# Transposes by matmul instead of by DMA, and buffer fills on the sync engine's queue, in a four-layer attention kernel ordered by a planner

## The chip, the cores and the metric

The kernel runs on one core of a Trainium2 chip. The core has TensorE (PE), VectorE (DVE), ScalarE (ACT), GpSimd (POOL) and the sync engine (SP); 16 DMA engines move data for all of them. A DMA issued by GpSimd goes to a software queue, one issued by the sync engine to a hardware queue. The metric is the device time of one execution in microseconds, as the median of several runs.

## The reference

Four layers run one after the other over x of 2048 rows by 512 columns in bf16: softmax attention A (32 query heads of width 16 that share one key and one value head), linear attention B, A again, B again. Each layer adds its output to x.

```python
def _A_ref(x, wq, wk, wv, wo):
    q = (x @ wq).reshape(B, S, H, Dh).transpose(0, 2, 1, 3)
    k = x @ wk
    v = x @ wv
    scores = jnp.einsum("bhqd,bkd->bhqk", q, k) * (Dh ** -0.5)
    p = _softmax(scores, axis=-1)
    o = jnp.einsum("bhqk,bkd->bhqd", p, v)
    return o.transpose(0, 2, 1, 3).reshape(B, S, H * Dh) @ wo
...
def _B_ref(x, wqkv, wo):
    ...
    phi = lambda t: jnp.where(t > 0, t + 1, jnp.exp(t)) + 1e-6
    pq, pk = phi(q), phi(k)
    kv = jnp.einsum("bhsd,bhse->bhde", pk, v)
    z = jnp.einsum("bhsd->bhd", pk)
    num = jnp.einsum("bhqd,bhde->bhqe", pq, kv)
    den = jnp.einsum("bhqd,bhd->bhq", pq, z)[..., None] + 1e-6
    ...
x = x + _A_ref(_layernorm(x, axis=-1), A_wq, A_wk, A_wv, A_wo)
x = x + _B_ref(_layernorm(x, axis=-1), B_wqkv, B_wo)
x = x + _A_ref(_layernorm(x, axis=-1), A_wq, A_wk, A_wv, A_wo)
x = x + _B_ref(_layernorm(x, axis=-1), B_wqkv, B_wo)
```

## The kernel before

The 2048 rows are 16 tiles of 128. All of x and the weights stay on the core.

**Attention (layers 0 and 2).** The scores of one tile of queries, half of the heads and one tile of keys are made in blocks of 128 by 512; a layer has 2048 blocks. A score matmul (`qk_mm`, L983) uses a quarter of TensorE's rows, so three or four blocks run side by side into PSUM banks. The exponential of a block is made on one of two engines:

- ScalarE takes most blocks, two or three at a time (L1163, the "doubles" and "triples" 128x1024 and 128x1536).
- VectorE takes the others by integer arithmetic: it adds a constant to the score and writes it as int16, whose bits read as bf16 are a power of two with a linear mantissa (L1249, one "block"). To mend the linear mantissa, three more copies of the block are wanted, each with another small constant added to the int16 (L1297, the "additions"), and the product with the values uses all four with four weights. Blocks are gathered by four into a "set" (`FB`, 128x2048), so an addition works on four blocks at once.

One of a set's three additions can be done by DMA instead of by VectorE: `prime` (L1309) fills a free buffer with the constant by a DMA that reads the row `shift_row` from DRAM (L1321, a "fill"), and `dma_shift` (L1328) later adds the set to it by an accumulating DMA (L1330). Both are issued by GpSimd. Whether a set goes that way is decided in `dve_shifts` (L1277): a fill must stand ready, the end of the layer must be more than `DMIN` segments away, and the planner's DMA backlog must be below `DQ`. A fill is started when fewer than `NPRE` stand ready and more than `FBP` buffers are free. Buffers lent by other tensors (`xn`, `wq`, `wo2`, `OBB`, `sacc`) serve as `FB` too, so a fill can have those names; the order prints `wo2` as `wo`.

The product with the values (L1037) reads what either engine or the DMA has made and sums in one PSUM bank. TensorE fills its gaps with matmuls that multiply by zeros (L1082 and L969, the "fillers"). At the end of a tile the sum is normalised into `Osb`, turned (`epilogue`, L1420) and projected (L754).

**Linear attention (layers 1 and 3).** Each tile of x is normalised (`ln_tile`, L826) into `xn`, turned into `xnT` and projected. Most of this runs beside the attention layer before it, as soon as that layer's tile is done.

**Turning a tile** is done in one of two ways. `dmat` (L760) issues a DMA transpose on the sync engine's queue. Or TensorE multiplies by the identity (L862 for `xn`, L1442 for `Osb`, four matmuls a tile) and ScalarE or VectorE copies the result from PSUM (L739). `FARA`, `FARB` and `FARO` say for which tiles the DMA is used.

**The order.** `Planner` (L36) simulates the engines with the costs written at each operation, and what comes out is each engine's fixed order of instructions; on the chip an engine runs its own order and waits on semaphores. A DMA's landing is modelled by one queue (`dmaq`, L193 to L203). While a transpose is under way no fill and no addition by DMA is dispatched (L158), and those that follow wait for the last transposes (L200):

```python
            if o.port and self.port > self.now or o.xfer and self.turning:
                held.append(x)
                continue
...
            if o.xfer:
                o.deps.update(self.turned)
                self.dmaq = max(end, self.dmaq) + o.xfer[0]
                end = self.dmaq + o.xfer[1]
```

`TUNE` replaces constants of the planner at the start of layer 0 and of layer 2.

Of the kernel before, what the change touches and what calls it, by code (L numbers as in the profile page):

```python
# [8 lines left out]
I16 = mybir.dt.int16  # L9
# [3 lines left out]
PE, AC, DV, PO, SP = "pe", "act", "dve", "pool", "sp"  # L13
ENGS = (PE, AC, DV, PO, SP)

P = 128
# [19 lines left out]
class Planner:  # L36
# [43 lines left out]
    def op(self, opts, reads=(), writes=(), prio=5.0, lat=0.08, dma=False, name="", join=None, mode="full", port=False, after=(), behind=(), xfer=None, trn=False):  # L80

        o = Op()
        o.opts, o.prio, o.users, o.done, o.end = opts, prio, [], False, None
        o.eng, o.fn, o.n, o.value, o.sem, o.signal, o.isdma = None, None, None, None, None, False, dma
        o.name = (name, lat)
        o.freed = False
        o.begun = None
        o.cols = 0
        o.mode = mode
        o.port = port  # L90
        o.xfer = xfer
        o.trn = trn
        deps = set()
        for k in reads:
            deps.update(self.ws(k))
        for k in list(writes) + list(after) + list(behind):
            deps.update(self.ws(k))
            deps.update(self.readers.get(k, ()))
        if join is not None:
            deps.update(join.deps)  # L100
            deps.discard(join)
        for k in writes:
            if join is not None and join in self.ws(k):
                self.writer[k] = self.ws(k) + [o]
            else:
                self.writer[k] = [o]
                self.readers[k] = []
        for k in list(reads) + list(after):
            if k not in writes:
                self.readers.setdefault(k, []).append(o)  # L110
        o.deps = deps
        o.left = 0
        chain = len(opts) == 1 and PE in opts
        for d in deps:
            if not (d.done or (chain and d.freed and d.eng == PE)):
                o.left += 1
                d.users.append(o)
        if o.left == 0:
            self._eligible(o)
        return o  # L120
# [26 lines left out]
    def _dispatch1(self, e):  # L147
# [4 lines left out]
        while h:  # L152
# [9 lines left out]
            if w:  # L162
                held.append(x)
                self.at(w, lambda: self._dispatch(e))
                break
            if e == PE and STICK and o.mode != "row" and o.mode != self.mode != "row":
                like = [y for y in h if y[2].eng is None and y[2].mode == self.mode and y[0] <= o.prio + STICK]
                if like:
# [187 lines left out]
class Seg:  # L356
# [11 lines left out]
    def take(self, js, back=False):  # L368
# [33 lines left out]
TRS = 1.4  # L402
TRT = 1.0
FARA = (4, 16)
FARB = 12
FARO = 12
FARM = {1: (), 3: ()}
GROW = (5,)
BLS = 1.4
BLO = 5.0  # L410
DXB = 2.0
# [13 lines left out]
ENDL = 12  # L425
# [6 lines left out]
CHB = 4  # L432
FBO = 2
FBS = 4
AHEAD = 20
CHT = 19
PSH = False
STICK = 1.5
PBL = 1.2
BACK = 2  # L440
PRING = 8
# [1 line left out]
DMIN = 4  # L443
NPRE = 2
EVEN = True
CHE = 8
AVOID = True
PGEN = 0.95
DPF = 1.75
DXF = 3.3  # L450
DTAIL = 2.0
DQ = 4.0
FBP = 4
TUNE = {0: {"CHE": 2, "CHT": 26, "FBP": 3, "ENDL": 16, "STICK": 0.8},
        2: {"CHE": 2, "FBO": 1, "AHEAD": 26, "BLS": 2.3, "DXB": 1.2, "NPRE": 3, "DMIN": 3, "STICK": 0.8}}


def bass_interleave_layers__grouped_kv_mqa__linear_attn_block__prompt_kernel(
# [12 lines left out]
    op = pl.op  # L471
# [39 lines left out]
    FB = sb("FB", [P, NFB, CHB * 512], BF16)  # L511
# [23 lines left out]
    pts, fbs = {}, {}  # L535
# [28 lines left out]
    def once(tag, keys):  # L564
        if tag in seen:
            return ()
        seen.add(tag)
        return keys

    def guest(L, kind, i, h=None):  # L570
        return once((L, kind, i, h), home[kind, i]) if (kind, i) in home else ()
# [10 lines left out]
    def bank_bf(i):  # L582
        return ps[:, i * 512:(i + 1) * 512].bitcast(BF16)[:, 0:512].rearrange("p (a b) -> p a b", a=4)
# [119 lines left out]
    cst = nc.dram_tensor("shift_row", (1, CHB * 512), I16, kind="Internal").ap()  # L703

    def fb_keys(i):
        return [("FB", i, h) for h in range(CHB)]
# [53 lines left out]
    def dmat(dst, src, reads, writes, prio, after=()):  # L760
        return op({SP: (0.1, lambda e: e.dma_start(dst, src, transpose=True))}, reads=reads, writes=writes, prio=prio, lat=0.5, dma=True, behind=after, trn=True)

    def until(*keys):
        for k in keys:
            yield ("ops", pl.ws(k))

    def halves(bs, dst, key, prio, psrc=None, after=()):
        l = op({DV: (DH_DUR, lambda e: e.tensor_copy(dst(0), psrc(bs[0], 0)))}, writes=[B_(bs[0]), key], prio=prio, behind=after)
        r = op({AC: (AH_DUR, lambda e: e.copy(dst(1), psrc(bs[1], 1)))}, writes=[B_(bs[1]), key], prio=prio, join=l, behind=after)
        pl.give_after(banks, bs[0], [l])  # L770
        pl.give_after(banks, bs[1], [r])
        return [l, r]
# [50 lines left out]
    def ring(L, t):  # L823
        return t % 4 if L == 3 else t
# [149 lines left out]
    def run_a(L):  # L974
# [23 lines left out]
        def spend(h, o):  # L998
            h[0] -= 1
            if o not in h[1]:  # L1000
                h[1].append(o)
            if h[0] == 0:
                pl.give_after(h[2], h[3], h[1])
# [85 lines left out]
        def act_stream():  # L1089
            if L == 0:  # L1090
                globals().update(TUNE[0])
            yield ("flag", ("K", L, 0))
            globals().update(TUNE[L])
            if L:
# [214 lines left out]
        def prime():  # L1309
            yield ("flag", ("K", L, T - 1))  # L1310
            if L == 0:
                row = FB[0:1, NFB - 1, :].bitcast(I16)
                op({DV: (0.6, lambda e: e.memset(row, DSH * 128 // NSH))}, writes=fb_keys(NFB - 1), prio=1.0)
                op({SP: (0.54, lambda e: e.dma_start(cst, row))}, reads=fb_keys(NFB - 1), writes=["cst"], prio=1.0, lat=2.5, dma=True)
            yield from until("cst")
            while state["si"] < len(segs) - DMIN:
                if len(primed) >= NPRE or len(fb_pool.free) <= FBP or fb_pool.wait:
                    yield ("sleep", 0.2)
                    continue
                g_ = yield ("acq", fb_pool, 9.0)  # L1320
                o = op({PO: (PGEN, lambda e, g_=g_: e.dma_start(fbs[g_].bitcast(I16), cst.to_broadcast([P, CHB * 512])))}, reads=["cst"], writes=fb_keys(g_), prio=9.0,  # L1321
                       lat=0.3, dma=True, behind=guest(L, "FB", g_), xfer=(DPF, DTAIL))
                primed.append((g_, o))
            while primed:
                g_, o = primed.pop()
                pl.give_after(fb_pool, g_, [o])

        def dma_shift(blk, f_, hold, g_, o):  # L1328
            pl.stat["dma"] += 1
            o = op({PO: (PGEN, lambda e: e.dma_start(fbs[g_].bitcast(I16), fbs[f_].bitcast(I16), accum_op=ALU.add))}, reads=fb_keys(f_), writes=fb_keys(g_), prio=0.0, lat=0.3,  # L1330
                   dma=True, xfer=(DXF, DTAIL))
            spend(hold, o)
# [32 lines left out]

        pl.process(spare())
        pl.process(prime())
        for i in pairs:
            pl.process(spare_sacc(i))
# [50 lines left out]
        def epilogue(t):  # L1420
# [5 lines left out]
            rd = [("Osb", k, 0), ("Osb", k, 1)]  # L1426
            if t >= FARO or t in ECRIT:
                yield from until(*rd)
            if t in ECRIT:
                bs = yield from acq2(pr)  # L1430
                o = tr2(src, rd, bs, pr)
                halves(bs, lambda h: dst[:, 2 * h:2 * h + 2, :], ("OT", m), pr, lambda b, h: bank_bf(b)[:, 0:2, :])
            elif t < FARO:
                o = dmat(dst, src, rd, [("OT", m)], pr)
# [50 lines left out]
    def run_b(L):  # L1485
# [45 lines left out]
        def tile_(t):  # L1531
            pr = base(t) + 0.01 * t
            yield ("flag", ("x", L - 1, t))
            yield from ln_tile(L, t, pr, t < FARB, t in ECRIT)
            c = ring(L, t)
# [398 lines left out]
```

## Time and profile before

| | us |
|---|---|
| median of 3 runs | 1499.13 |
| lowest and highest | 1496.74 and 1501.04 |
| the profiled execution | 1500.94 |
| its span, first to last instruction | 1499.2 |
| busy: ScalarE, TensorE, VectorE, GpSimd | 1448.2, 1424.7, 1406.7, 358.7 |

The profile is of one execution. Busy time is the time in which at least one instruction of the engine is under way; instructions of an engine overlap a little at their ends, so a row's mean duration is longer than the distance from one start to the next. An idle time in a row's brackets is that of the engine just before the row, with what ended it. A transpose or load on the sync engine's queue is written SPq. The stages by time: layer 0's attention to about 715 us with layer 1 partly beside it, the rest of layer 1 and the start of layer 2 to about 840 us, layer 2's attention with layer 3 beside it to about 1461 us, then the rest of layer 3.

### The profile page before, as it was taken

The page shows a single profiled execution, that of the slowest core. Times are in us where ns is not written, and L with a number is a line of the kernel's source. Part 1 is how long each engine was busy: PE and PEld are TensorE (multiplying, and loading weights), DVE is VectorE, ACT ScalarE, POOL GpSimd, SP SyncE. Part 2 cuts the span into 40 slices and gives each one's busy share as a digit, 9 for nine tenths or more (in the row PEclk, how much of TensorE's full clock was granted, in tenths as well). Part 3 has the DMA queues.
Part 4 walks back from the last instruction along what each step waited for, and adds up shares of the span by engine and source line. Part 5 has one row for each costly group of instructions (what it writes and reads, how often), then busy time and mean ns, then how long its engine had stood idle before and what let it go on. Part 6 is the DMA issues. An engine that isn't in the chain of part 4 may idle for free. (4 is left out here: it accounts for less than half of the span.)

```text
span 1499.2 us, 40089 instructions
## 1 busy us (share of the span) xinstructions
PE 1424.7 (95%) x16261; PEld 511.2 (34%) x16261; DVE 1406.7 (94%) x2594; ACT 1448.2 (97%) x1510; POOL 358.7 (24%) x537
## 2 busy tenths in 40 slices
PE   7999999989999999999999999999899999999998
PEld 4433332323233323333644333333233323333335
DVE  7999989989999999999767799999999999999996
ACT  8999999989999999999699999999999999999996
POOL 5322222212232222100111222222222223223001
PEclk9999999999999999999999999999999999999999
DMA  5867777767668878500000577586976877788101
GB/s 118 222 163 150 153 161 174 155 134 170 143 159 186 183 153 200 121 30 2 1 2 1 128 173 156 138 177 156 169 169 155 183 150 174 173 177 209 33 2 57
DMA packets 91480, 200.81 MB, mean 134 GB/s; under 512 B 39713, under 2 KB 46369, under 8 KB 91298
## 3 DMA queue, kind: packets, MB, share of 16 engines
q0 software_dynamic: 49968, 181.95, 53.1%
q1 hardware_dynamic: 41330, 16.30, 5.6%
q8 instruction: 130, 2.13, 0.6%
q14 instruction: 52, 0.43, 0.1%
HBM read 98.60 MB, written 2.10 MB: 67 GB/s over the span
## 5 line engine op out<-in xcount | busy, mean ns | idle before, releaser
L1163 ACT ACTIVATE PT<-ps 128x1024 bf16<-128x1024 f32 (+1 forms) x947 | 1002.4, 1171 | 8.2 <-PE ps L983 6.6
L983 PE MATMUL ps<-QT,KM 32*128 32x512 bf16 x4096 | 538.5, 385 | 21.8 <-ACT PT L1163 12.1
L1249 DVE TENSOR_SCALAR FB<-ps 128x512 int16<-128x512 f32 x785 | 515.2, 679 | 17.7 <-PE ps L983 16.9
L1037 PE MATMUL ps<-FB,VW 128*32 128x512 bf16 x3179 | 431.3, 385 | 12.5 <-DVE sacc L1383 2.8
L1037 PE MATMUL ps<-PT,V 128*32 128x512 bf16 x2109 | 349.1, 387 | 17.9 <-ACT PT L1163 7.5
L983 PEld LDWEIGHTS ps<-QT,KM 32*128 32x128 bf16 x4096 | 135.2, 91 | 443.6 <-ACT PT L1163 205.0
L1163 ACT ACTIVATE xnT<-ps 128x1024 bf16<-128x1024 f32 (+1 forms) x235 | 249.5, 1136 | 3.3 <-PE ps L983 2.8
L1297 DVE TENSOR_SCALAR FB<-FB 128x2048 int16<-128x2048 int16 (+1 forms) x331 | 220.3, 674 | 0.6
L1163 ACT ACTIVATE OBB<-ps 128x1024 bf16<-128x1024 f32 (+1 forms) x166 | 183.7, 1164 | 8.2 <-PE ps L983 8.0
L1330 POOL DMA_DIRECT2D FB<-FB x89 | 88.6, 1005 | 329.4 <-DVE FB L1249 179.6
L1082 PE MATMUL ps<-QT,V 128*32 128x512 bf16 (+6 forms) x680 | 161.9, 317 | 0.5 <-DVE FB L1249 0.5
L1037 PEld LDWEIGHTS ps<-FB,VW 128*32 128x32 bf16 x3179 | 106.4, 94 | 134.1 <-issue 73.8
L1321 POOL DMA_DIRECT2D FB<-shift_row x130 | 109.5, 874 | 92.0 <-PE ps L1037 46.3
L1037 PEld LDWEIGHTS ps<-PT,V 128*32 128x32 bf16 x2109 | 85.0, 93 | 97.9 <-issue 41.3
L1037 PE MATMUL ps<-xnT,V 128*32 128x512 bf16 x511 | 103.3, 387 | 3.1 <-ACT xnT L1163 1.9
L837 POOL TENSOR_SCALAR ve<-mv 128x1 f32<-128x1 f32 x64 | 27.0, 424 | 327.0 <-DVE mv L836 325.5
L754 PE MATMUL ps<-wqkv,xnT 128*32 128x512 bf16 x960 | 85.6, 390 | 0.3 <-DVE xnT L739 0.2
L1037 PE MATMUL ps<-OBB,V 128*32 128x512 bf16 x368 | 77.9, 388 | 1.5 <-DMA xn<-FB 0.6
L1082 PEld LDWEIGHTS ps<-QT,V 128*32 128x32 bf16 x680 | 53.8, 95 | 71.9 <-issue 48.3
L1249 DVE TENSOR_SCALAR wo<-ps 128x512 int16<-128x512 f32 x80 | 53.0, 680 | 3.5 <-PE ps L983 3.2
L1037 PE MATMUL ps<-xn,VW 128*32 128x512 bf16 x271 | 55.9, 384 | 0.3 <-DMA FB<-FB 0.2
L1383 DVE COPY sacc<-ps 128x512 f32<-128x512 f32 x64 | 43.5, 679 | 9.1 <-PE ps L1037 8.9
(225 smaller groups left out, 1787.3 us busy)
## 6 DMA issues: line engine op xcount, KB each, us to landing
FB<-shift_row POOLq DMA_DIRECT2D x130, 512.0 KB, 6.9
FB<-FB POOLq DMA_DIRECT2D x89, 512.0 KB, 5.8
FB<-wo POOLq DMA_DIRECT2D x13, 512.0 KB, 5.5
xn<-shift_row POOLq DMA_DIRECT2D x11, 512.0 KB, 7.4
sacc<-shift_row POOLq DMA_DIRECT2D x9, 512.0 KB, 7.7
wo<-shift_row POOLq DMA_DIRECT2D x9, 512.0 KB, 7.5
FB<-OBB POOLq DMA_DIRECT2D x9, 512.0 KB, 5.8
OBB<-shift_row POOLq DMA_DIRECT2D x9, 512.0 KB, 7.2
```

The costliest lines, as they stand in the source:

```text
L754: ins = e.matmul(dst[c, :], lhsT=l[:, c], rhs=r, start=(k == 0), stop=(k == len(pairs) - 1))
L837: op({PO: (0.1, lambda e: e.tensor_scalar(out=ve[:, t:t + 1], in0=mv[:, t, 1:2], scalar1=1e-5, scalar2=None, op0=ALU.add))}, reads=[("mv", ...
L983: return e.matmul(bank(b), lhsT=KM[r, sg.par, kt * P:(kt + 1) * P], rhs=QT[r, sg.t, :], start=True, stop=True)
L1037: ins = e.matmul(ps[32 * j:32 * j + 32, ACC * 512:(ACC + 1) * 512], lhsT=V[:, kt, :] if w is None else VW[:, kt, w, :], rhs=ap, start=(k = ...
L1082: o = op({PE: (n / 2400.0, lambda e: e.matmul(ps[32 * j:32 * j + 32, b * 512:b * 512 + n], lhsT=V0[:], rhs=QT[:, sg.t, 0:n], start=st, sto ...
L1163: ex = op({AC: (0.051 + 0.4267 * n, lambda e, n=n, s_=s_, p_=p_: e.activation(pts[p_][:, 0:n * 512], ps[:, s_ * 512:(s_ + n) * 512], ACTF. ...
L1249: o = op({DV: (0.602, lambda e: e.tensor_scalar(out=dst.bitcast(I16), in0=bank(b), scalar1=VB, scalar2=VLO, op0=ALU.add, op1=ALU.max))}, w ...
L1297: o = op({en: (du, lambda e, w=w, g_=g_: e.tensor_scalar(out=fbs[g_][:, 0:n].bitcast(I16), in0=fbs[f_][:, 0:n].bitcast(I16), scalar1=float ...
L1321: o = op({PO: (PGEN, lambda e, g_=g_: e.dma_start(fbs[g_].bitcast(I16), cst.to_broadcast([P, CHB * 512])))}, reads=["cst"], writes=fb_keys ...
L1330: o = op({PO: (PGEN, lambda e: e.dma_start(fbs[g_].bitcast(I16), fbs[f_].bitcast(I16), accum_op=ALU.add))}, reads=fb_keys(f_), writes=fb_k ...
L1383: o = op({DV: (0.6, lambda e, src=src: e.tensor_copy(src, bank(ACC)))}, writes=[B_(ACC), key], prio=0.0, lat=0.15, behind=host(L, key) if ...
```

## The change

`FARB` and `FARO` go to 0: the first twelve tiles of each B layer and of each attention output, which were turned by DMA, are turned by TensorE with a copy by VectorE or ScalarE. `FARA` stays, so the twelve DMA transposes at the start of layer 0 remain. The fills are issued by the sync engine instead of GpSimd. Besides, constants of the planner change: its costs of a fill and of an addition by DMA, the bonus for staying in one mode of TensorE, and the values set for each layer, of which only `DMIN` is left.

```diff
-FARB = 12
-FARO = 12
+FARB = 0
+FARO = 0
...
-STICK = 1.5
+STICK = 0.8
...
-DPF = 1.75
-DXF = 3.3
+DPF = 1.7
+DXF = 3.2
...
-TUNE = {0: {"CHE": 2, "CHT": 26, "FBP": 3, "ENDL": 16, "STICK": 0.8},
-        2: {"CHE": 2, "FBO": 1, "AHEAD": 26, "BLS": 2.3, "DXB": 1.2, "NPRE": 3, "DMIN": 3, "STICK": 0.8}}
+TUNE = {0: {"DMIN": 2},
+        2: {"DMIN": 2}}
...
-                o = op({PO: (PGEN, lambda e, g_=g_: e.dma_start(fbs[g_].bitcast(I16), cst.to_broadcast([P, CHB * 512])))}, reads=["cst"], writes=fb_keys(g_), prio=9.0,
-                       lat=0.3, dma=True, behind=guest(L, "FB", g_), xfer=(DPF, DTAIL))
+                o = op({SP: (0.54, lambda e, g_=g_: e.dma_start(fbs[g_].bitcast(I16), cst.to_broadcast([P, CHB * 512])))}, reads=["cst"], writes=fb_keys(g_), prio=9.0,
+                       lat=0.2, dma=True, behind=guest(L, "FB", g_), xfer=(DPF, DTAIL))
```

In numbers of instructions over the whole order: fills 176 to 218, additions by DMA 171 to 214, DMA transposes 60 to 12, matmuls that turn a tile (L862 and L1442) 120 to 312, additions of a full set on VectorE 654 to 626, blocks on VectorE 1108 to 1127, triples and doubles on ScalarE 293 to 241 and 1054 to 1123, fillers (L1082) 680 to 596.

## The prediction

> **What bounds the kernel now.** I read the page first, then the windows by stage, then the places in which all engines lost time at once, and last the transfers that stand there. The page's first part gives busy time, share of the span and number of instructions:
>
> ```profile
> PE 1424.7 (95%) x16261; PEld 511.2 (34%) x16261; DVE 1406.7 (94%) x2594; ACT 1448.2 (97%) x1510; POOL 358.7 (24%) x537
> ```
>
> Three engines are nearly full, GpSimd is not. The windows tell more; the columns are PE, PEld, DVE, ACT and POOL busy, the granted clock, the DMA share and GB/s:
>
> ```profile
> core 0: us, PE busy (x) PEld busy (x) DVE busy (x) ACT busy (x) POOL busy (x), PEclk, DMA share, GB/s
> 175.00:200.00 25.00, 21.66 (x233) 6.44 (x233) 21.27 (x39) 22.06 (x22) 6.39 (x9) 0.93 0.82 156
> 300.00:325.00 25.00, 19.14 (x203) 5.81 (x204) 19.97 (x37) 19.52 (x19) 6.16 (x9) 0.93 0.69 138
> 325.00:350.00 25.00, 23.59 (x265) 7.00 (x257) 22.79 (x40) 23.20 (x24) 3.83 (x5) 0.94 0.60 139
> 400.00:425.00 25.00, 24.35 (x294) 7.64 (x290) 24.97 (x45) 25.00 (x28) 6.34 (x8) 1.00 0.74 164
> 450.00:475.00 25.00, 23.49 (x269) 7.42 (x266) 24.99 (x44) 24.81 (x25) 7.36 (x9) 1.00 0.91 195
> 750.00:775.00 25.00, 24.32 (x299) 11.40 (x296) 17.43 (x37) 24.66 (x25) 3.01 (x9) 1.00 0.01 2
> 1050.00:1075.00 25.00, 21.28 (x258) 7.29 (x258) 22.50 (x42) 22.62 (x25) 6.39 (x10) 1.00 0.81 153
> ```
>
> The row of 400 us is the ordinary one: in the attention stages ScalarE and VectorE are both full, since they share the exponentials, and either can set the pace. Around 750 us, between those stages, VectorE has 7.6 us in 25 to spare. Four windows (175, 300, 325, 1050) lose time on ScalarE, VectorE and TensorE together: on ScalarE 2.9 + 5.5 + 1.8 + 2.4 = 12.6 us. These are three stalls. The row of 450 us has the DMA engines at 0.91 and loses nothing, so a full DMA alone is not the cause. The timeline at the three places shows GpSimd's additions (L1330), the transposes on the sync engine's queue (L761) and TensorE:
>
> ```profile
> 180.90 1.30 POOL L1330 DMA_DIRECT2D FB<-FB  x1 [0.52 <-DVE FB L1249]
> 180.94 1.20 SPq L761 DMA_TRANSPOSE xnT<-xn  x1
> 190.74 0.39 PE L1037 MATMUL ps<-PT,V 128*32 128x512 bf16 x2 [2.44 <-DMA FB<-FB]
> ...
> 310.03 0.89 POOL L1330 DMA_DIRECT2D FB<-FB  x1 [1.42 <-DVE FB L1249]
> 310.07 1.19 SPq L761 DMA_TRANSPOSE xnT<-xn  x1
> 320.71 0.86 POOL L1330 DMA_DIRECT2D FB<-FB  x1 [9.80 <-DMA xnT<-xn]
> 322.32 0.61 PE L1037 MATMUL ps<-PT,V 128*32 128x512 bf16 x1 [5.00 <-DMA FB<-FB]
> ...
> 1053.00 0.89 POOL L1330 DMA_DIRECT2D OBB<-FB  x1 [0.22 <-issue]
> 1053.04 1.19 SPq L761 DMA_TRANSPOSE xnT<-xn  x1
> 1063.50 0.39 PE L1037 MATMUL ps<-FB,VW 128*32 128x512 bf16 x1 [2.51 <-DMA OBB<-FB]
> ```
>
> Each time an addition is issued and a transpose 0.04 us behind it, and TensorE then waits for that addition: 2.44, 5.00 and 2.51 us. The view of line L1330 (who waited for it, and the time from issue to landing) says how special these three are. The first two lines are of all 171 additions, the next three of windows that hold the three late ones alone:
>
> ```profile
>   PE ps L1037: 11.3, 7
> DMA to landing us min/median/max: 4.5/5.8/12.2
> ...
> DMA to landing us min/median/max: 9.8/9.8/9.8
> ...
> DMA to landing us min/median/max: 12.2/12.2/12.2
> ...
> DMA to landing us min/median/max: 10.5/10.5/10.5
> ```
>
> They landed after 9.8, 12.2 and 10.5 us where the median is 5.8, and of the 11.3 us that TensorE waited for additions in all, 9.95 are theirs. The planner holds an addition back while a transpose is under way, but not a transpose behind an addition that has just gone.
>
> **The change, part by part.** The predicted time is made against the profiled run, 1500.94 us (span 1499.2 and 1.7 around it); that is 1.8 above the median of 1499.13.
>
> *Transposes leave the DMA queue (48 of 60; the 12 left lie in the first 45 us, before any addition).* GpSimd's queue at the stall of 310 us stands so before; sp12 is the transpose's semaphore, pool1 to pool7 and pool0 are those of its own transfers:
>
> ```order
> L837 TENSOR_SCALAR ve<-mv 128x1 [waits s_dve]
> L839 TENSOR_TENSOR rs<-ve,mhalf 128x1 [waits s_pool]
> L1321 DMA wo<-shift_row 128x2048 [waits s_pe]
> L1330 DMA FB<-FB 128x2048 [waits s_dma_pool1,s_dma_pool5,s_dve]
> L1330 DMA FB<-FB 128x2048 [waits s_dma_pool6,s_dma_pool2,s_dve,s_dma_sp12]
> L1330 DMA wo<-FB 128x2048 [waits s_dma_pool0,s_dve]
> L1321 DMA wq<-shift_row 128x2048 [waits s_dma_pool4,s_pe]
> L1321 DMA FB<-shift_row 128x2048 [waits s_pe]
> ```
>
> And so it stands in the middle of the same stage in the changed kernel, where each sp semaphore is that of a fill:
>
> ```order
> L837 TENSOR_SCALAR ve<-mv 128x1 [waits s_dve]
> L839 TENSOR_TENSOR rs<-ve,mhalf 128x1 [waits s_pool]
> L1330 DMA xn<-sacc 128x2048 [waits s_dma_pool6,s_dma_sp7,s_dve]
> L1330 DMA FB<-FB 128x2048 [waits s_dma_pool7,s_dma_sp8,s_dve]
> L1330 DMA FB<-FB 128x2048 [waits s_dma_pool0,s_dma_sp9,s_dve]
> L1330 DMA FB<-sacc 128x2048 [waits s_dma_pool1,s_dma_sp10,s_dve]
> ```
>
> The fills (L1321) and the waits on transposes are gone from this queue; an addition now waits for its fill on the other queue. With no transpose beside it the three stalls have no cause: the four windows go back to the usual 0.1 us of loss each, 12.6 - 0.4 = **-12.2 us**. At least, by TensorE's own three waits, it is -9.95.
>
> *Transposes on TensorE.* In the changed order of TensorE, at a transpose of attention's output (L1442) among the score matmuls (L983), the products (L1037) and the fillers (L1082):
>
> ```order
> L983 MATMUL ps<-QT,KM 128x512 x3
> L1037 MATMUL ps<-OBB,V 32x512
> L1037 MATMUL ps<-PT,V 32x512 x3
> L983 MATMUL ps<-QT,KM 128x512 x3
> L1442 MATMUL ps<-ident,Osb 128x128 x4
> L1037 MATMUL ps<-FB,VW 32x512 x12
> L983 MATMUL ps<-QT,KM 128x512 x3
> ```
>
> Four matmuls stand between two score groups. Their price, and the fillers that they displace:
>
> ```profile
> L862 PE MATMUL ps<-ident,xn 128*128 128x128 bf16 x96 | 9.9, 229 | 6.4 <-DVE xn L842 5.6 <-DVE sacc L1249 0.5 <-DVE QT L1494 0.3
> ...
> L1082 PE MATMUL ps<-QT,V 128*32 128x512 bf16 (+6 forms) x680 | 161.9, 317 | 0.5 <-DVE FB L1249 0.5
> ```
>
> A tile costs 9.9/24 = 0.41 us, 48 tiles 20 us. Fillers compute nothing and fall from 680 to 596 in the order, 84 x 161.9/680 = 20 us. So TensorE is even, **0**; the cover is that a score group is ready one exponential (0.9 us, below) ahead. Without it each tile would cost its 0.41, 20 us at most.
>
> *ScalarE and VectorE.* Durations are from start to start where instructions follow each other (ScalarE, then VectorE, then the two copies by group):
>
> ```profile
> 308.39 1.06 ACT L1163 ACTIVATE PT<-ps 128x1024 bf16<-128x1024 f32 x1
> 309.29 1.50 ACT L1163 ACTIVATE OBB<-ps 128x1536 bf16<-128x1536 f32 x1
> 310.62 2.45 ACT L1163 ACTIVATE PT<-ps 128x1024 bf16<-128x1024 f32 x2
> ...
> 561.27 0.68 DVE L1297 TENSOR_SCALAR FB<-FB 128x2048 int16<-128x2048 int16 x1
> 561.87 0.68 DVE L1249 TENSOR_SCALAR wo<-ps 128x512 int16<-128x512 f32 x1
> 562.47 0.68 DVE L1249 TENSOR_SCALAR FB<-ps 128x512 int16<-128x512 f32 x1
> ...
> L739 DVE COPY xnT<-ps 128x512 bf16<-128x512 bf16 x19 | 7.9, 413 | 4.6 <-PE ps L862 4.6
> L739 ACT COPY xnT<-ps 128x512 bf16<-128x512 bf16 x5 | 3.1, 629 | 0.0
> ```
>
> A double exponential takes 0.90 us, a triple 1.33, a block or an addition on VectorE 0.60. Counted over the whole order, ScalarE goes from 293 triples to 241 (-69 us) and from 1054 doubles to 1123 (+62), and gains 12 copies at most 0.63 each (+7.5) less a few casts (-3.5): about -4 us, spread over both stages. VectorE gains 19 blocks (+11.4), loses 28 long additions (-16.8) though GpSimd's additions rise by 43 (171 to 214), because more blocks mean more sets to be weighted, and gains 36 copies at most 0.41 each (+14.8) and some casts and short additions (+2.5): about +12. By place: +7 in the first attention stage, +5 in the stretch between, where it has room (0), -4 in the second stage and +4 behind the last block. So by ScalarE alone the plan gains 4, by VectorE alone it loses 7; as both are full I take the mean, (-4 + 7)/2 = **+1.5**.
>
> *Fills to the sync engine's queue, additions 171 to 214.* Rows: the page on the queues and on fills, and from the views of L1321 (fills) and L672 (loads by the sync engine) the time to landing:
>
> ```profile
> q0 software_dynamic: 49968, 181.95, 53.1%
> q1 hardware_dynamic: 41330, 16.30, 5.6%
> ...
> L1321 POOL DMA_DIRECT2D FB<-shift_row x130 | 109.5, 874 | 92.0 <-PE ps L1037 46.3 <-DMA xnT<-xn 13.3 <-DVE FB L1297 13.0
> ...
> DMA to landing us min/median/max: 3.7/7.0/10.4
> ...
> DMA to landing us min/median/max: 2.1/3.9/7.3
> ```
>
> GpSimd gets 176 x 0.87 us back, which bounds nothing. q0 holds 176 fills and 171 additions: 0.531 x 1499.2 = 796 us, 2.3 each. 85 more are +195 us, the transposes take at most 84 away: the share goes from 59% to 66%. The window of 450 us shows 0.91 at no loss, so load itself is 0. Lateness other than the three stalls was 11.3 - 9.95 = 1.35 us of TensorE for 168 additions, for 214 it is 1.7: **+0.4**. Before, fills and additions stood in one queue, in turn; now a fill of the other queue can come in beside an addition. No row shows that pair. The nearest rows are an addition behind others in its own queue (median 5.8, no loss) and one beside a transpose (up to 12.2); a fill is a plain transfer of the kind whose loads land in 3.9, so I take the first and keep the second for a rival. [...]
>
> Sum: 1500.94 - 12.2 + 1.5 + 0.4 = 1490.6 profiled; less 1.8, **1489 us** by the median. Its own range: 9.95 to 12.6 for the stalls, -4 to +7 for the pace: 1484 to 1497.
>
> **The rivals.** *Fills make additions late (slower).* Mechanism: a fill issued while an addition is under way shares the DMA engines with it and adds up to its 2.3 us to 4.5 to 5.8, and TensorE, which takes its work in order, stands at the product that reads it, with the next score groups behind it, for which ScalarE and VectorE wait. For: the three stalls are just this pair with a transpose in the fill's place, and now 218 fills run there instead of 48 transposes. Against: 5.8 + 2.3 = 8.1 is still short of the 9.8 that cost 2.44. At the smallest stall's 2.44 us, five late additions of 214 eat the gain; at one in twenty, 11 x 2.44 = 26, it is 1515. *VectorE's pace takes the gain (no change).* If the +12 all lay on the path, -12.2 + 12 + 0.4 leaves 1499. For: VectorE is at 24.97 of 25 in the ordinary window. Against: 5 of the 12 lie where it has room. *It doesn't do what it says:* the order holds 218 fills on the sync engine's queue, 214 additions on GpSimd's and 48 more transposes on TensorE, so this has no chance.
>
> **How the numbers follow.** Forecast 0.58, late additions 0.24, pace 0.13, and 0.05 for a time under 1484. About 0.3% (4.5 us) is what a measurement of this kernel can tell from no change, so faster means below 1494.6. Of the forecast's 0.58, 0.54 lie below that; with the 0.05, faster is 0.59. The pace case and the forecast's rest give 0.14 the same, the remainder and the late additions 0.27 slower. The range leaves out a tenth at each end: below, 1479; above, near the late additions' own time, 1513.
>
> **What would show it.** Right: no window of the attention stages with ScalarE below 24 of 25; waits of TensorE for additions under 3 us in all; no addition landing past 9.5 us; fillers near 140 us busy; transposes on TensorE near 0.41 us a tile. Wrong: many waits of TensorE for an addition of 0.5 to 3 us each with a fill issued just before it lands (late additions); or none of those and ScalarE idle for TensorE's scores while VectorE stands at 25 of 25 (pace).

## The result

The changed kernel takes 1513.91 us (median; 1506.86 to 1520.47) against 1498.2 for the kernel before (1496.74 to 1501.04): a ratio of 1.0105, interval 1.0075 to 1.0134. It is slower by 15.7 us where the forecast was 1489. The profiled execution took 1511.93 us.

The page of the changed kernel, busy times and the two queues:

```profile
PE 1435.5 (95%) x16434; PEld 520.2 (34%) x16434; DVE 1417.8 (94%) x2625; ACT 1447.6 (96%) x1531; POOL 286.3 (19%) x404
...
q0 software_dynamic: 30816, 112.21, 40.4%
q1 hardware_dynamic: 46610, 124.31, 24.5%
```

ScalarE is busy for 1447.6 us, as before (1448.2), in a span 11 us longer: it has no more to do, it waits more. The windows (columns as in the prediction) show where; the first three are those of the old stalls:

```profile
175.00:200.00 25.00, 24.27 (x286) 7.75 (x283) 24.98 (x46) 25.00 (x27) 5.91 (x7) 1.00 0.83 190
300.00:325.00 25.00, 23.59 (x272) 7.45 (x276) 24.89 (x46) 24.97 (x28) 5.61 (x7) 1.00 0.89 193
1050.00:1075.00 25.00, 24.34 (x278) 8.58 (x280) 24.83 (x46) 24.69 (x27) 4.91 (x6) 1.00 0.75 184
...
425.00:450.00 25.00, 22.58 (x246) 7.02 (x242) 23.36 (x44) 23.31 (x24) 4.65 (x6) 1.00 0.76 171
475.00:500.00 25.00, 21.28 (x234) 6.13 (x233) 20.80 (x38) 20.97 (x24) 2.78 (x3) 0.93 0.66 160
1225.00:1250.00 25.00, 22.66 (x238) 6.49 (x237) 21.52 (x40) 21.60 (x23) 4.58 (x7) 0.93 0.79 190
```

The three stalls are gone: ScalarE loses 0.0, 0.03 and 0.3 us there. Others have come, the largest at 425, 475 and 1225 us, with 1.7, 4.0 and 3.4 us of ScalarE lost. The view of line L1330 tells who waited for the additions, and how long they took to land:

```profile
  PEld ps L1037: 30.8, 34
  PE ps L1037: 20.7, 24
...
DMA to landing us min/median/max: 4.4/5.9/9.8
```

TensorE waits 24 times for an addition where it waited 7 times before (20.7 us against 11.3), and its weight loads 34 times. Yet the median landing is 5.9 us against 5.8: the additions are not slower on the whole, some of them are. The timeline at the largest of these waits:

```profile
477.48 1.02 POOL L1330 DMA_DIRECT2D FB<-FB  x1 [4.78 <-DVE FB L1249]
477.51 0.80 SPq L1321 DMA_DIRECT2D FB<-shift_row  x2
...
487.29 0.40 PE L1037 MATMUL ps<-FB,VW 128*32 128x512 bf16 x4 [2.96 <-DMA FB<-FB]
```

The addition is issued at 477.48, two fills on the sync engine's queue 0.03 and 0.5 us behind it, and the addition lands 9.8 us after its issue. The DMA view gives each queue's packets, MB and share of the engines; the first line is of 478 to 482 us, the second of 484 to 488:

```profile
q1 hardware_dynamic: 227, 0.86, 84.8%
...
q0 software_dynamic: 208, 0.76, 96.4%
```

From 478 to 482 there is no row for q0 at all: not a byte of the addition moves while the two fills, issued behind it, have the engines. They have overtaken it. The timeline's rows suggest why: GpSimd needs 1.02 us to issue the addition, the sync engine 0.80 for both fills. Experiments 5 and 9 test it.

The wait itself is not all that is lost. The windows of 2 us around it, columns as above (the granted clock is the third number from the end):

```profile
484.00:486.00 2.00, 0.34 (x6) 0.04 (x3) 2.00 (x5) 1.55 (x2) 0.00 (x0) 1.00 1.04 209
488.00:490.00 2.00, 2.00 (x22) 0.42 (x23) 0.34 (x1) 1.72 (x2) 0.00 (x0) 0.59 0.12 23
490.00:492.00 2.00, 2.00 (x23) 0.48 (x19) 0.97 (x3) 0.70 (x2) 0.00 (x0) 0.56 0.00 0
```

After the wait of 2.96 us TensorE is busy without a gap, but at a granted clock of 0.59 and 0.56, and VectorE and ScalarE still stand idle for 2.7 and 1.6 of these 4 us. After the wait at 425 us, of 1.59 us, the clock stays at 1.00.

### The profile page after: what moved, and what is told of

Read it like the earlier page. It is cut to its first block, busy times and chain, and to the rows that moved or that the text cites. A ratio compares the mean times of both kernels' runs of the same rounds, so it can differ in the third digit from the quotient of the medians.

```text
span 1510.1 us, 40679 instructions
## 1 busy us (share of the span) xinstructions
PE 1435.5 (95%) x16434; PEld 520.2 (34%) x16434; DVE 1417.8 (94%) x2625; ACT 1447.6 (96%) x1531; POOL 286.3 (19%) x404
## 4 chain that ended last, share of the span: by engine, by line
PE 31%; issue 22%; DVE 18%; ACT 15%; DMA 9%; POOL 5%; POOLq 0%; ACTq 0%; DVEq 0%
PE ps L1037 11%; ACT PT L1163 10%; PE ps L983 9%; DVE FB L1249 7%; DMA FB<-FB 4%; DVE FB L1297 3%; PE ps L754 2%; PE ps L1082 2%; POOL FB L1330 2%; ACT OBB L1163 2%; ACT xnT L1163 2%; PE ps L916 2%; PE ps L1403 1%; DMA OBB<-FB 1%; PE ps L750 1%
## 5 line engine op out<-in xcount | busy, mean ns | idle before, releaser
L1249 DVE TENSOR_SCALAR FB<-ps 128x512 int16<-128x512 f32 x800 | 526.9, 682 | 16.7 <-PE ps L983 15.3
L1037 PE MATMUL ps<-FB,VW 128*32 128x512 bf16 x3250 | 462.8, 386 | 18.2 <-DMA FB<-FB 6.2
L1037 PE MATMUL ps<-PT,V 128*32 128x512 bf16 x2101 | 381.9, 387 | 7.0 <-ACT PT L1163 2.2
L1330 POOL DMA_DIRECT2D FB<-FB x116 | 111.6, 962 | 460.6 <-DVE FB L1249 404.7
L1082 PE MATMUL ps<-QT,V 128*32 128x512 bf16 (+6 forms) x596 | 145.3, 316 | 0.6 <-DVE FB L1249 0.4
L1037 PEld LDWEIGHTS ps<-PT,V 128*32 128x32 bf16 x2101 | 93.6, 93 | 81.7 <-issue 38.1
L1037 PE MATMUL ps<-xnT,V 128*32 128x512 bf16 x507 | 114.3, 389 | 6.5 <-DMA FB<-FB 3.7
L1082 PEld LDWEIGHTS ps<-QT,V 128*32 128x32 bf16 x596 | 47.4, 95 | 63.6 <-issue 42.5
L1037 PE MATMUL ps<-sacc,VW 128*32 128x512 bf16 x252 | 55.4, 384 | 0.3 <-ACT PT L1163 0.2
L1037 PE MATMUL ps<-wo,VW 128*32 128x512 bf16 x263 | 53.0, 384 | 1.3 <-DMA wo<-FB 1.3
L1037 PE MATMUL ps<-OBB,VW 128*32 128x512 bf16 x240 | 49.8, 385 | 3.0 <-DMA OBB<-FB 1.2
```

What stands on the lines that cost most here:

```text
L1037: ins = e.matmul(ps[32 * j:32 * j + 32, ACC * 512:(ACC + 1) * 512], lhsT=V[:, kt, :] if w is None else VW[:, kt, w, :], rhs=ap, start=(k = ...
L1082: o = op({PE: (n / 2400.0, lambda e: e.matmul(ps[32 * j:32 * j + 32, b * 512:b * 512 + n], lhsT=V0[:], rhs=QT[:, sg.t, 0:n], start=st, sto ...
L1249: o = op({DV: (0.602, lambda e: e.tensor_scalar(out=dst.bitcast(I16), in0=bank(b), scalar1=VB, scalar2=VLO, op0=ALU.add, op1=ALU.max))}, w ...
```

## The experiments

Two theories at the start. **Lateness:** fills on a queue of their own make single additions later than the plan holds them, and TensorE stands at their products. **Pace:** the new order itself is longer, by VectorE's added work or the transposes on TensorE. In the recorded expectations these are L and P; L1 is lateness by the two queues, L2 lateness by load.

**1 and 2. Nothing waits for an addition.** Same orders on all engines, but the product with a part made by DMA reads a constant tile (`wkr`); the corrections by DMA are left out. The next fill of such a buffer then has no such product to wait for either; what that is worth was not separated. Once on the kernel after, once on the kernel before:

```diff
-pv_post(o, [(sg, kt, j, fbs[g_][:, h * 512:(h + 1) * 512], ("FB", g_, h)) ...
+pv_post(o, [(sg, kt, j, wkr[:].rearrange("p f d -> p (f d)"), "wkr") ...
```

> The changed kernel, every engine's order the same, but the products of the parts that the DMA adds read a constant tile (wkr) in place of the filled buffer, so TensorE waits for no addition; all fills and additions still run. It leaves the corrections of these parts out. Theory L (late additions cost the time): the waits of TensorE for additions (20.7 us) and what they cost go, 1484 to 1494 us, about 20 less than the changed kernel. Theory P (the new order itself is slower: more small exponentials, more work on VectorE, transposes on TensorE): 1503 to 1514, at most 10 less.

> The kernel before with the same edit: orders the same, TensorE waits for no addition. Both theories: the three stalls go, about 10 to 13 us less than before, 1485 to 1489 us. The difference between this and the changed kernel with the same edit is the price of the order alone: near 0 to +3 by theory L, +12 or more by theory P. If this one stays at 1498, the three stalls were not worth what the prediction put on them.

The kernel after gives 1489.64 us (ratio to the kernel before 0.9948, 0.9928 to 0.9968), the kernel before 1489.39 (0.9945, 0.9927 to 0.9964). Without lateness the two orders differ by 0.25 us, less than the intervals. Pace falls. All lateness of the kernel before, the three stalls included, was worth 1497.82 - 1489.39 = 8.4 us (5.4 to 10.9 by the interval).

**3 and 4. The same order with one queue, and the kernel after again beside it.** The planner's result is kept for TensorE, VectorE and ScalarE; the fills are only moved into GpSimd's list, each at the time at which the plan had it:

```diff
+    def queues(self):
+        fills = [setattr(o, "eng", PO) or o for o in self.order[SP] if o.xfer]
+        self.order[SP], self.order[PO] = [o for o in self.order[SP] if not o.xfer], sorted(self.order[PO] + fills, key=lambda o: o.t0)
...
-        allops = [o for e in ENGS for o in self.order[e]]
+        allops = self.queues() or [o for e in ENGS for o in self.order[e]]
```

> The changed kernel with the fills issued by GpSimd, each at its planned place among the additions, so fills and additions stand in one software queue again; the orders of TensorE, VectorE and ScalarE stay the same. Theory L by interleaving of two queues (L1): additions land sooner, TensorE waits for them under 8 us, 1490 to 1502 us. Theory L by load or tight costs (L2: 25% more additions and a plan that expects them too soon): the waits stay at 20 us or grow with GpSimd's 0.87 us a fill, 1512 to 1525. Theory P: 1510 to 1516.

> The changed kernel as it is, on the same chip as the three others, to be compared with: 1507 to 1520 us by all theories.

With one queue it takes 1491.23 us (0.9952, 0.9935 to 0.997), the kernel after beside it 1520.27 (1.0152, 1.012 to 1.0183). Line L1330 with one queue, and the same addition as above with the next fill:

```profile
  PEld ps L1037: 3.6, 12
  PE ps L1037: 0.2, 1
...
DMA to landing us min/median/max: 4.5/6.1/8.9
...
476.19 1.02 POOL L1330 DMA_DIRECT2D FB<-FB  x1 [4.79 <-DVE FB L1249]
477.20 0.58 POOL L1321 DMA_DIRECT2D FB<-shift_row  x1
```

And of the kernel after in this series:

```profile
  PEld ps L1037: 35.0, 38
  PE ps L1037: 24.1, 29
...
DMA to landing us min/median/max: 4.4/6.1/9.4
```

TensorE's waits go from 24.1 us to 0.2, though the additions land after the same 6.1 us in the median. The addition at 476.19 now lands in 5.6 us: its fill is issued behind it and stays behind. Issue by issue, in the first profile of the kernel after: of 214 additions 43 have a fill issued between 0.6 us ahead and 0.55 us behind them; these land after 7.3 us in the median and 11 of them after more than 8, the other 171 after 5.7 with 5 over 8. Of TensorE's 24 waits 19 are for these 43 additions, 16.9 of the 20.7 us. With one queue the same 43 land after 5.7 us in the median, and one after more than 8. So the 29 us between the two runs are those of the second queue; load falls as a cause, since both runs make the same transfers. What lateness costs the kernel after is 1520.27 - 1489.64 = 30.6 us in this series (23.5 by the ratios of the first). Why the same kernel takes longer in this series is not shown, but its granted clock goes with it: in the first series 1506.86 us at 0.999 and 1520.47 at 0.991, here 1515.03 at 0.995 and 1526.92 at 0.989, and with one queue 0.998 to 1.000.

**5. The pair by itself.** A small program issues transfers of the kernel's size, 12 times for each case, and leaves the kernel's work out:

> Transfers alone: 128x2048 additions and fills without the computation (the output is a copy of x). Twelve times each: an addition alone; a fill alone on the sync engine's queue; an addition with one fill, and with two, on the sync engine's queue right behind it; an addition with a fill on GpSimd's own queue right behind it, and right ahead of it; two additions on GpSimd's queue; an addition with a DMA transpose right behind it. Theory L1 (the two queues are served by turns): the addition alone lands in about 4.5 us, with a fill behind it on the other queue 1.5 to 2.5 us later, with two 3 to 5 later, but with a fill behind it on its own queue within 0.5 us of the addition alone. Theory L2 (load and a tight plan, no matter which queue): a fill behind it on its own queue costs it as much as one on the other. The transpose: 9 to 12 us, as in the three stalls.

The landings of the addition, in this order: alone; with one fill of the sync engine issued 0.3 us ahead (it was meant to be right behind); with two, 0.3 us ahead and 0.1 us behind; with a fill on its own queue behind; with one on its own queue 0.6 us ahead; with a DMA transpose 0.2 us ahead:

```profile
DMA to landing us min/median/max: 4.5/4.5/4.6
...
DMA to landing us min/median/max: 6.3/6.5/6.6
...
DMA to landing us min/median/max: 8.6/8.8/8.9
...
DMA to landing us min/median/max: 5.4/5.5/5.5
...
DMA to landing us min/median/max: 5.2/6.5/6.6
...
DMA to landing us min/median/max: 4.5/4.9/5.1
```

One fill ahead adds 2.0 us, whichever queue it is on, and two of the sync engine add 4.3, though the second is issued behind the addition; a fill behind on the addition's own queue adds 1.0, where L1 had at most 0.5. The packet records tell why the second comes first: a fill of the sync engine with nothing ahead of it moves its first packet 0.95 us after its issue, an addition with nothing ahead of it 1.43 us after. By these a fill issued up to 0.48 us later is out first, and 24 of the 43 additions above have such a fill behind them (13 of TensorE's 24 waits, 13.5 us, are for these). The case with a transpose was a miss: 0.4 us more, where the three stalls had led me to expect a late addition.

**6. Order kept by a wait.** In the kernel after each fill also waits until the last addition planned before it has landed:

```diff
+    def queues(self):
+        for o in [o for o in self.order[SP] if o.xfer]:
+            o.deps.update([a for a in self.order[PO] if a.xfer and a.t0 <= o.t0][-1:])
```

> The changed kernel, same orders, fills on the sync engine's queue, but each fill also waits until the last addition planned before it has landed, so none comes in beside an addition under way. Theory L1: the waits of TensorE for additions fall from 20-24 us to under 8, 1491 to 1500 us (a late fill may hold back an addition in its turn). Theory L2: they stay, 1510 to 1525.

1514.66 us (1.0117, 1.0088 to 1.0147): no gain. Line L1330, the last row what GpSimd waited for ahead of its additions:

```profile
  PE ps L1037: 16.9, 19
...
  DMA FB<-shift_row: 70.2, 18
```

Fills that wait for a landing come late themselves, and GpSimd stands 70.2 us for them. The lateness was moved, so this run does not decide between L1 and L2; its time lies in the range of L2, against which experiment 3 speaks.

**7 and 8. Replanned with the old queue, or with a margin.** Seven has the line of the fill as it was before the change, on GpSimd; eight keeps the fills on the sync engine's queue and lets the planner hold a landing to be 2 us later (`DTAIL` is what it adds behind a transfer):

```diff
-DTAIL = 2.0
+DTAIL = 4.0
```

> The changed kernel with the one line of the fill as before (issued by GpSimd, planned so); transposes on TensorE and the new constants stay. 208 additions. Theory L1: near the changed kernel with the queues joined afterwards (1491), 1488 to 1495. Theory L2: 1505 to 1520. It is also the candidate for a kernel that beats both.

> The changed kernel with the planner's tail of a transfer at 4.0 us instead of 2.0 (DTAIL), so that a product is ordered later after its addition; fills stay on the sync engine's queue. Theories L1 and L2 alike: additions land as late as before but TensorE asks for them later, so its waits fall under 8 us; 1492 to 1502. If it stays above 1508, the waits are not a matter of the plan's margin.

Seven: 1495.24 us (0.9989, 0.9971 to 1.0008), no difference from before and just above the 1488 to 1495 expected: with the old queue the rest of the change, planned so, gains nothing that is clear of noise. Eight: 1491.13 (0.9966, 0.9948 to 0.9983), with 211 additions and these waits:

```profile
  PE ps L1037: 0.2, 1
...
DMA to landing us min/median/max: 4.5/6.0/9.9
```

The longest landing is 9.9 us, as in the kernel after, and costs nothing: the products stand later in TensorE's order. Not the landing costs here, but the landing against the plan. Three and eight both beat the kernel before and the kernel after. Three lies within 2 us of what its order gives with no lateness; for the order of eight that was not measured.

**9. Who goes first.** The small program again, with the fill issued when the addition is out, and the trio of the three stalls:

> The disputed cost by itself again, now with the fill issued when the addition is already out; an addition alone took 4.5 us and 6.5 with a fill of the other queue beside it. If the DMA engines take from the two queues by turns (theory L), the addition lands at 5.5 to 6.5 us with one fill issued behind it on SP's queue and at 7 to 9 with two, at 5.0 to 5.7 with two fills behind it on its own queue; of an addition, a fill and a second addition the second lands later than on one queue only if the turns favour the fill. If what counts is only who comes first (rival), an addition that is out first stays at 4.5 to 5 in all. For the three stalls of the kernel before: a fill on the own queue ahead and a transpose beside should give 9 or more if these together were their cause; the single pairs gave 6.5 and 4.9, so 7 if they only add up.

The addition's landings: one fill of the sync engine issued 1.1 us behind it; two; two on its own queue; a fill on its own queue 0.6 us ahead and a transpose with it; the second of two additions with a fill of the sync engine between them; the same three on one queue:

```profile
DMA to landing us min/median/max: 5.4/5.5/5.6
...
DMA to landing us min/median/max: 5.5/5.5/5.5
...
DMA to landing us min/median/max: 5.5/5.6/5.6
...
DMA to landing us min/median/max: 8.8/10.7/11.7
...
DMA to landing us min/median/max: 8.9/9.1/9.4
...
DMA to landing us min/median/max: 8.1/8.4/8.7
```

An addition that is out first pays 1.0 us for what follows, one fill or two, on either queue. L1, "by turns", predicted 7 to 9 for two fills on the sync engine's queue: a miss. Its rival, that only the first counts, predicted 4.5 to 5 and is half a microsecond short. What counts most in these cases is who is out first: 6.5 us with the fill ahead, 5.5 with it behind. The trio lands after 10.7 us, where its pairs gave 6.5 and 4.9. That is near the landings of the three stalls, and a fill does stand ahead of each in the kernel before:

```profile
179.76 0.61 POOL L1321 DMA_DIRECT2D FB<-shift_row  x1
...
307.89 0.71 POOL L1321 DMA_DIRECT2D wo<-shift_row  x1
...
1052.15 0.62 POOL L1321 DMA_DIRECT2D FB<-shift_row  x1
```

**10. The stalls of the kernel before.** There, each DMA transpose also waits for the last addition planned before it (the edit of experiment 6, for transposes):

> The kernel before with each DMA transpose also made to wait for the last addition that the plan issued before it. If a transpose issued 0.04 us behind an addition is what makes it late (the prediction's reading of the three stalls), the landings of 9.8 to 12.2 us go, and the time is 1488 to 1493 unless the transposes, now later, hold up those that read them. If the transpose was not the cause, additions still land past 9.5 us at the same places and the time is 1497 to 1500.

1505.75 us (1.0048, 1.0019 to 1.0078). The window of the first stall, TensorE's waits for additions, and from the view of the transposes' line L761 what GpSimd's additions waited for them:

```profile
175.00:200.00 25.00, 23.54 (x277) 7.42 (x269) 25.00 (x46) 25.00 (x26) 8.14 (x9) 1.00 0.63 149
...
  PE ps L1037: 12.0, 15
...
  POOL FB L1330: 162.7, 20
```

The late landings go (at most 8.1, 7.8 and 7.7 us around the three places, though two of 10.4 and 10.5 come elsewhere). The first stall goes with them and most of the second (ScalarE loses 0.6 us of the 5.5 at 300 us); at 1050 us 1.8 of the 2.4 us stay lost though no landing there is that late. So the transpose was part of the cause of the late landings. The time is missed: the transposes now come late, GpSimd stands for them (162.7 us against 115.7 before), and TensorE waits 15 times for additions instead of 7.

**11. The fills alone.** The kernel before with only the fills on the sync engine's queue, planned anew: 170 additions, 60 DMA transposes.

```diff
-                o = op({PO: (PGEN, lambda e, g_=g_: e.dma_start(fbs[g_].bitcast(I16), ...
-                       lat=0.3, ...
+                o = op({SP: (0.54, lambda e, g_=g_: e.dma_start(fbs[g_].bitcast(I16), ...
+                       lat=0.2, ...
```

> The kernel before with the fills alone moved to SP's queue and planned anew (170 additions, 175 fills, 60 DMA transposes stay). If the fills on a second queue are what costs (theory L), TensorE waits some 25 us and more for additions in 15 or more waits, and the time is 1505 to 1525. If it is the other parts of the change (more additions, other constants, transposes on TensorE), it stays at 1495 to 1501.

1581.4 us (1.0551, 1.05 to 1.0601), with these waits for additions:

```profile
  PE ps L1037: 53.6, 32
...
DMA to landing us min/median/max: 4.5/6.4/11.8
```

This one part costs 84 us alone, more than either expectation had, at the lowest granted clock of all runs (0.969 to 0.976). It is the harmful part of the change. Beside the 60 transposes it costs more than in the kernel after; whether by the trio or by the fills and transposes standing in one list on the sync engine was not separated.

**12. More additions under a margin.** The kernel after with `DTAIL` 3.5 and the backlog `DQ` 6.0, which gives 233 additions:

> The kernel after with the plan's margin behind a transfer raised from 2.0 to 3.5 us and the backlog that it allows from 4.0 to 6.0, so that 233 additions are issued in place of 214; 4.0 of margin alone gave 1491.1. If lateness against the plan is all that costs (theory L), the margin covers it, each of the 19 additions more frees 0.6 us of VectorE, of which about half shows since ScalarE is as full, and the time is 1482 to 1489. If load decides (rival), the added additions land late at any margin and the time is 1492 to 1505.

1507.27 us (1.0073, 1.005 to 1.0097), a miss for the theory, and above the 1492 to 1505 of its rival too. TensorE waits little for additions (view of L1330); GpSimd's additions wait for fills (view of L1321):

```profile
  PE ps L1037: 4.6, 4
...
  POOL FB L1330: 33.4, 6
```

With the deeper backlog late fills hold additions back, 6 times and 33.4 us in all. How this and the few waits make up 16 us over experiment 8 stays open.

## Why the prediction was wrong

**The stalls (-12.2): right in place, too large.** They went, but experiment 2 puts all lateness of the kernel before at 8.4 us. The time that ScalarE loses in these windows (12.6 us) overstates what its removal is worth; where the rest is made up was not shown. The cause was only half read: beside a transpose alone an addition lands after 4.9 us, with a fill in front of both after 10.7.

**Transposes on TensorE (0) and pace (+1.5): right in sum; singly they were not measured.** Groups of the kernel after:

```profile
L862 PE MATMUL ps<-ident,xn 128*128 128x128 bf16 x192 | 19.5, 225 | 5.8 <-DVE xn L842 5.6
...
L1082 PE MATMUL ps<-QT,V 128*32 128x512 bf16 (+6 forms) x596 | 145.3, 316 | 0.6 <-DVE FB L1249 0.4
```

19.5/48 = 0.41 us a tile, and the fillers at 145.3 us have made room. The whole order apart from lateness came out at +0.25 us, by experiments 1 and 2. Two slips in the adding are small: ScalarE's terms make -3, not -4, and the range's own low end comes to 1483.

**Fills to the sync engine's queue (+0.4): the step that failed.** It scaled the 1.35 us of other waits from 168 additions to 214. Measured, lateness costs the kernel after 24 to 31 us; that is more than TensorE's 20.7 and 24.1 us of waits. The low clock behind the wait of 2.96 us (0.59 and 0.56), which the term did not have, is by the author's estimate a part of the difference; it was not sized. "No row shows that pair": of the two nearest rows I took the addition behind others in its own queue, and it was the wrong one. In its own queue an addition has issued ahead of it only what the plan put there (6.5 us with one fill ahead, 5.5 with one behind, in experiment 5). Across the two queues the addition landed after 6.5 us where a fill was out ahead of it and after 5.5 where it was out first (experiments 5 and 9), and a fill of the sync engine is out sooner (0.95 us after its issue against 1.43). With measured terms, -8.4 + 0.25 + 24 to 31 = +16 to +23, against +15.7 in the first series and +22.5 in the second; this closes by construction, since the last term was taken from the same times. The check of its own is experiment 3: without the second queue 29 us go.

**The first rival was the truth.** Its price, 1515 us, is near the measured 1513.9. Its mechanism was right in place and effect; its count was not: not 11 waits of 2.44 us but 24 of 0.86 in the mean on TensorE, and a fill adds 2.0 us by being ahead, not by sharing: q0 had nothing for 4 us (478 to 482) while q1 served two fills, and an addition with two fills behind it lands after 5.5 us, as with one. That the price fits so well is partly luck: it took 26 us of waiting for 20.7 that cost more than their length, and -12.2 for the stalls where experiment 2 gives -8.4. What was said against it, that 8.1 us is short of 9.8, took one late landing's length for a threshold. The plan has its own landing for each addition, and experiment 8 shows 9.9 us costing nothing.

## What to carry to other kernels

When an order is planned with one queue in mind, moving some of its transfers to another queue can change who goes first, as it did here at equal load and an equal median landing of 6.1 us (experiments 3 and 4): look for pairs issued close together (a fill up to 0.48 us behind an addition, by the first packets here), and price them by the case where the other transfer wins (6.5 us here against 4.5 alone). To tell lateness from pace, let the consumers read a constant and keep every order; the difference of two runs sizes it. If transfers may overtake, move the consumers back in the plan (1491.13 us here) or keep one queue (1491.23); a wait between the queues only moved the lateness (1514.66).

## What the runs showed of the hardware

A DMA transpose alone beside an addition costs it 0.4 us (4.9 against 4.5), but with a fill ahead of both the addition lands after 10.7 us. In one case of experiment 9 the DMA view shows q0 from 341.2 to 342.2 us, when 3 packets of the transpose move, and both queues later, from 344.2 to 349.2 us (the share adds up the packets' own times, so it can pass 100%):

```profile
q0 software_dynamic: 81, 0.32, 106.2%
...
q0 software_dynamic: 94, 0.34, 45.8%
q1 hardware_dynamic: 225, 0.05, 7.5%
```

The fill and the addition move 0.32 MB in one microsecond, and then 0.34 MB in five, while the transpose sends 225 small packets of 0.2 KB in the mean. The transpose itself lands after 10.5 us instead of 3.1 (medians). Also unexpected: an addition with a fill close behind lands 1.0 us later even on its own queue (5.5 against 4.5), and a second fill behind adds nothing on the sync engine's queue (5.5) and 0.1 on its own (5.6); with another addition 0.5 us behind it lands after 4.6 us, as good as alone.
